# Pairing the blocks: two first products, then two second products, in a fused attention and feed-forward kernel

## The chip, the cores and the metric

One core of a Trainium2 chip runs the kernel. The metric is the device time of one execution in microseconds, the median of three. PE is TensorE (matmul), PEld its weight loads, DVE is VectorE, ACT ScalarE, POOL GpSimd, SP SyncE, whose queue issues the DMAs.

## The reference

Sparse attention over 8 batches, 8 heads, 576 tokens and head size 64, and a feed-forward layer on its output (4608 tokens, 512 channels, 2048 hidden), all in float32:

```python
scores = scale * np.matmul(q, k.transpose(0, 1, 3, 2))
mask_local = (rel >= 0) & (rel < stride)                # heads 0 to 3, stride 32
mask_strided = (rel >= 0) & (pos[None, :] % stride == pos[:, None] % stride)   # heads 4 to 7
attn = softmax(where(mask, scores, -1e9)); x = attn @ v   # tokens x 512
h = x @ w_in
g = 0.5 * h * (1.0 + erf(h * inv_sqrt2))
return (g @ w_out)
```

## The kernel before

**Tiles and steps.** The 4608 tokens are cut into 12 tiles of 384 (`TT`), the hidden layer into 16 blocks of 128 (`NF`). A step n is one hidden block of one tile (t = n // 16, f = n % 16); there are 192 (`NS`). Float32 products are made of three: each factor is split into a high part and a rest (`xh`, `xl`; `gh`, `gl`; `w[:, 0]`, `w[:, 1]`), and three of the four products of parts are added.

- `ffn_h(n)` (L645 to L647) is the first product of a step, called H here: 12 matmuls of 384 columns into one PSUM bank. There are two such banks (`ps_h`, bufs=2), so H(n+2) writes the bank of H(n).
- `ffn_g(n)` is what follows on it: gelu in place (ACT, L654), the cast to `gh` (ACT, L656) and the subtract to `gl` (DVE, L658), which is the last to read the bank. `gh` and `gl` have three buffers each (`gpool`, bufs=3).
- `ffn_o(n)` (L684 to L686) is the second product, called O: 9 matmuls of 512 columns, three into each of three banks that add up over the 16 steps of a tile. `store(t)` (L691) copies the three banks on ACT and sends them out.

**Attention beside it.** The local heads of a tile are three jobs (`band_job`), each in numbered parts: 0 scores (PE, L322), 1 mask and maximum (DVE, L336), 2 exponentials (ACT, L340), 3 sum, quotient, transpose and eight small DMAs (DVE L343 to L346, SP L351), 4 the product with v (PE, L362), 5 and 6 the split into `xh` and `xl` (ACT L263, DVE L265). Parts 4 of one tile and 0 of the next stand together in a *visit*, once a tile. `value_at` and `score_at` say at which step; `soft_at` spreads parts 1 to 3 of the three jobs over the steps behind it. `load_keys` and `load_values` ask for the next tile's data on SP, each held until a gelu named by the caller.

The strided heads are done on DVE alone, as a list of small operations (L520 products, L562 sums) in order (`strided`). `run_strided(upto)` issues the list as far as a planned sum of costs; what a step gets follows from the time left to the tile that needs it, less `taken`, the planned cost of the local heads' vector work. Their exponentials on ACT (L530) wait in `exps` until `flush_exps`; finished outputs wait in `splits` for their split into `xh` and `xl`.

**Order.** An opening (`START`, a list written by hand) loads and splits the weights and does the first 16 steps. From step 16 on `step(n)` is called for each n: visit if there is one, H(n) with all of `ffn_g(n)`, loads, splits, `softmaxes(n)`, the strided share, then O(n−2). On PE this reads H(n), O(n−2), H(n+1), O(n−1), and so on. ACT and PE keep the written order (`manual_schedule`); DVE, POOL and SP are ordered by the scheduler's own timeline. After step 191 one more region does O(190) and O(191) together, bank by bank.

Of the kernel before, what the change touches and what calls it, by code (L numbers as in the profile page):

```python
# [46 lines left out]
NB = 16  # L47
# [35 lines left out]
def attn_ffn_kernel(ctx: ExitStack, tc: tile.TileContext, qk, vl, qka, va, qs, ks, vs, w, out):  # L83
# [6 lines left out]
    NF = w.shape[0]  # L90
    NC = DM // P
    NU = len(PLACE)
    NV = len(VISITS)
    NTILE = NT // TT
    NS = NTILE * NF
    JPT = NJ // NTILE
# [30 lines left out]
    def slot(name, shape, dtype=F32):  # L127

        return wpool.tile(shape, dtype, name=name, tag="w")
# [58 lines left out]
    def set_jq(x):  # L188
        jq[x] = qbig[:, x % JPT]

    def set_jv(x):
        jv[x] = vbig[:, x % JPT].rearrange("p (a h d) -> p a h d", a=2, h=HL)
# [13 lines left out]
    def load_keys(t, after):  # L206

        js = range(t * JPT, (t + 1) * JPT)
        ins = nc.sync.dma_start(qbig, qk[js[0]:js[0] + JPT].rearrange("j p c -> p j c"))
        for x in js:  # L210
            set_jq(x)
        tc.add_manual_dep(ins.ins, after.ins.name, mybir.DependencyInfo(
            mybir.DependencyClass.Sync, mybir.DependencyReason.DATA), reason="pace")

    def load_values(t, after):

        js = range(t * JPT, (t + 1) * JPT)
        ins = nc.sync.dma_start(vbig, vl[js[0]:js[0] + JPT].rearrange("j p a h d -> p j (a h d)"))
        for x in js:
            set_jv(x)  # L220
        tc.add_manual_dep(ins.ins, after.ins.name, mybir.DependencyInfo(
            mybir.DependencyClass.Sync, mybir.DependencyReason.DATA), reason="pace")
# [81 lines left out]
    def score_banks(t):  # L304
        return [ps_a.tile([P, DM], F32, name=f"S{j}_{t}", tag=f"S{j}") for j in range(2)]
# [166 lines left out]
    for vi in range(NA, NV):  # L472
        n = VISITS[vi][2]
# [26 lines left out]
    exps, splits = [], []  # L500

    def flush_exps(u):
        while exps and exps[0][0] <= u:
            exps.pop(0)[1]()
# [131 lines left out]
    hps, gs, ops_, gelu = {}, {}, {}, {}  # L636
    ready = [t * NF for t in range(NTILE)]
    xfree = [0, 0] + ready[1:-1]

    def ffn_h(n):  # L640
        t, f = divmod(n, NF)
        xh, xl = xt[t]
        hp = ps_h.tile([P, TT], F32, name=f"H_{n}", tag="H")
        for c in range(NC):
            nc.tensor.matmul(hp, w1[f][:, 0, c, :], xh[:, c, :], start=(c == 0), stop=False)  # L645
            nc.tensor.matmul(hp, w1[f][:, 0, c, :], xl[:, c, :], start=False, stop=False)  # L646
            nc.tensor.matmul(hp, w1[f][:, 1, c, :], xh[:, c, :], start=False, stop=(c == NC - 1))  # L647
        hps[n] = hp

    def ffn_g(n):  # L650
        hp = hps.pop(n)
        gh = gpool.tile([P, TT], F32R, name=f"gh_{n}", tag="gh")
        gl = gpool.tile([P, TT], F32R, name=f"gl_{n}", tag="gl")
        gelu[n] = nc.scalar.activation(hp, hp, AF.Gelu)  # L654
        yield
        nc.scalar.copy(gh, hp)  # L656
        yield
        nc.vector.tensor_tensor(gl, hp, gh.bitcast(F32), ALU.subtract)  # L658
        gs[n] = (gh, gl)

    def runs(t, a):

        res = []
        for c in range(0, P, 32):
            _, b, r = ROWS[TR * t + (a * P + c) // 32]
            r = b * S + 32 * r
            if res and res[-1][2] + res[-1][1] - res[-1][0] == r:
                res[-1][1] = c + 32
            else:
                res.append([c, c + 32, r])  # L670
        return res

    def ffn_o(*ns):

        t = ns[0] // NF
        if ns[0] % NF == 0:
            ops_[t] = [ps_o.tile([P, DM], F32, name=f"O_{t}_{a}", tag=f"O{a}") for a in range(TT // P)]
        for a in range(TT // P):
            o = ops_[t][a]
            sl = slice(a * P, (a + 1) * P)  # L680
            for n in ns:
                f = n % NF
                gh, gl = gs[n]
                nc.tensor.matmul(o, gh[:, sl], w2[f][:, 0, :], start=(f == 0), stop=False)  # L684
                nc.tensor.matmul(o, gh[:, sl], w2[f][:, 1, :], start=False, stop=False)  # L685
                nc.tensor.matmul(o, gl[:, sl], w2[f][:, 0, :], start=False, stop=(f == NF - 1))  # L686

    def store(t):
        for a in range(TT // P):
            ob = opool.tile([P, DM], F32, name=f"ob_{t}_{a}", tag="ob", bufs=3)  # L690
            nc.scalar.copy(ob, ops_[t][a])  # L691
            for c0, c1, r0 in runs(t, a):
                nc.sync.dma_start(out[r0:r0 + c1 - c0, :], ob[c0:c1, :])
# [5 lines left out]
    for u in range(U0, NU + 1):  # L699
        for v, what, names in ((u, strided_qk, "qk"), (u - 1, strided_av, "v")):  # L700
            if U0 <= v < NU:
                vi, _, r0, nr, t, _ = PLACE[v]
# [11 lines left out]
    def run_strided(upto):  # L714
        while pos[0] < len(strided) and cum[pos[0]] <= upto + 1e-9:
            if strided[pos[0]][1] == 0.6 and len(splits) >= 3:
                break
            strided[pos[0]][2]()
            pos[0] += 1

    for h in range(HL):
        m = smask[h * 32:(h + 1) * 32]
# [19 lines left out]
    t = slot("pbig", [P, 4 * DM])  # L742
# [27 lines left out]
    for i in range(JPT):  # L770
        t = opool.tile([P, DM], F32, name=f"first_{i}", tag="ob", bufs=3)
# [51 lines left out]

    FIRST, VISIT, DELAY = 2, 13, 1
    value_at = {ready[t - 1] + VISIT: t for t in range(2, NTILE)}
    score_at = {ready[1] + FIRST: 2, **{n: t + 1 for n, t in value_at.items()}}
    soft_at = {}
    for n, t in score_at.items():  # L830
        for i in range(JPT if t < NTILE else 0):
            for p in (1, 2, 3):
                soft_at.setdefault(n + p + i * (2 if t == 2 else 4), []).append((t * JPT + i, p))

    taken = [2.2 * (n in value_at) + sum({1: 0.66, 3: 1.2}.get(p, 0) for _, p in soft_at.get(n, ()))
             for n in range(NS + 2)]
# [7 lines left out]
    def part(x, *which):  # L844

        for p in which:
            if p == 0:
                local[x] = [band_job(x, bts[x % NBT], banks), 0]
            assert local[x][1] == p
            local[x][1] += 1  # L850
            next(local[x][0], None)

    def visit(n):

        t = value_at.get(n, 0)
        if score_at.get(n, 0):
            banks[score_at[n]] = score_banks(score_at[n])
        for i in range(JPT if t else 0):
            part(t * JPT + i, 4)
        for i in range(JPT if score_at.get(n, NTILE) < NTILE else 0):  # L860
            part(score_at[n] * JPT + i, 0)

    def softmaxes(n):

        t = value_at.get(n, 0)
        for p in (5, 6) if t else ():
            for i in range(JPT):
                part(t * JPT + i, p)
        for x, p in soft_at.get(n, ()):
            if p == 2:  # L870
                flush_exps(NU)
            part(x, p)

    def step(n):


        c = n // NF
        visit(n)
        if NB <= n < NS:
            ffn_h(n)  # L880
            for _ in ffn_g(n):
                pass
        if n - DELAY in score_at and score_at[n - DELAY] + 1 < NTILE:
            load_keys(score_at[n - DELAY] + 1, gelu[n])
        if n - DELAY in value_at and value_at[n - DELAY] + 1 < NTILE:
            load_values(value_at[n - DELAY] + 1, gelu[n])
        old = len(splits)
        while old and n >= xfree[splits[0][0]]:
            for _ in splits.pop(0)[1]():
                pass  # L890
            old -= 1
        softmaxes(n)
        flush_exps(NU)
        if c + 1 < NTILE:
            a, e = ready[c] + (1 if c == 0 else 0), ready[c + 1]
            part_of = min(1.0, max(0.0, (n - a + 1) / (e - a - 3)))
            need = last[c] + (last[c + 1] - last[c] + sum(taken[a:e - 3])) * part_of - sum(taken[a:min(n + 1, e - 3)])
            share = (n + 1 - NB) / (ready[-1] - 2 - NB)
            run_strided(max(need, (tot + sum(taken)) * share - sum(taken[:n + 1])))
        if n == NS + 1:  # L900
            ffn_o(n - 3, n - 2)
        elif n >= NB + 2 and n < NS:
            ffn_o(n - 2)
        if n >= NB + 2 and (n - 2) % NF == NF - 1:
            store((n - 2) // NF)

    with tc.manual_schedule(engines={ET.Activation, ET.PE}):
        for n in range(NB, NS + 1):
            step(n)
    with tc.manual_schedule(engines={ET.Activation, ET.PE}):  # L910
        step(NS + 1)


def lay_out(q, k, v, w_in, w_out):
# [62 lines left out]
```

## Time and profile before

| | |
|---|---|
| median of 3 runs | 874.68 us (874.24 to 876.21) |
| the profiled execution | 874.25 us, span 872.5 us |
| PE, PEld busy | 855.5, 769.5 us |
| DVE, ACT, POOL busy | 705.9, 483.2, 17.5 us |
| granted TensorE clock, mean | 0.994 |

The span is what the profile sees from the first to the last instruction. Rows of groups give line, engine, operation, output and inputs by name with their shapes, count, then busy time and mean ns of one, then idle time before them and what ended it. Rows of the timeline give start and length in us, engine, line and operation. Rows of stretches give start:end, length, busy time of PE, PEld, DVE, ACT and POOL, the granted clock, the DMA share and GB/s. Rows of waits give who waited for whom: total us, times, longest. Rows of DMA issues give count, KB each and us to landing.

### The profile page before, as it was taken

The page shows a single profiled execution, that of the slowest core. Times are in us where ns is not written, and L with a number is a line of the kernel's source. Part 1 is how long each engine was busy: PE and PEld are TensorE (multiplying, and loading weights), DVE is VectorE, ACT ScalarE, POOL GpSimd, SP SyncE. Part 2 cuts the span into 40 slices and gives each one's busy share as a digit, 9 for nine tenths or more (in the row PEclk, how much of TensorE's full clock was granted, in tenths as well). Part 3 has the DMA queues.
Part 4 walks back from the last instruction along what each step waited for, and adds up shares of the span by engine and source line. Part 5 has one row for each costly group of instructions (what it writes and reads, how often), then busy time and mean ns, then how long its engine had stood idle before and what let it go on. Part 6 is the DMA issues. An engine that isn't in the chain of part 4 may idle for free.

```text
span 872.5 us, 19562 instructions
## 1 busy us (share of the span) xinstructions
PE 855.5 (98%) x6082; PEld 769.5 (88%) x6082; DVE 705.9 (81%) x4901; ACT 483.2 (55%) x1001; POOL 17.5 (2%) x89
## 2 busy tenths in 40 slices
PE   6899999999999999999999999999999999999998
PEld 5788899899899899899899989989989989989997
DVE  5988999998989997889999979899799995751111
ACT  6978586476466466356455546547536535543222
POOL 5000100000000000000000000000000000000000
PEclk9799999999999999999999999999999999999999
DMA  9696210420310150030122121122014003000001
GB/s 345 231 353 229 91 48 19 128 76 8 116 56 9 33 169 8 18 121 19 56 76 73 56 75 48 35 67 98 13 30 141 17 8 93 12 7 16 22 0 37
DMA packets 33976, 66.67 MB, mean 76 GB/s; under 512 B 6224, under 2 KB 15952, under 8 KB 33872
## 3 DMA queue, kind: packets, MB, share of 16 engines
q1 hardware_dynamic: 33872, 65.43, 22.4%
q8 instruction: 48, 0.79, 0.4%
q14 instruction: 56, 0.46, 0.2%
HBM read 51.64 MB, written 9.44 MB: 70 GB/s over the span
## 4 chain that ended last, share of the span: by engine, by line
PE 90%; DMA 4%; DVE 2%; ACT 1%; SPq 1%; issue 1%; ACTq 0%
PE H L645 15%; PE O L685 15%; PE O L686 15%; PE H L647 14%; PE H L646 14%; PE O L684 14%; DMA ws<-in_w_dram 2%; PE X_L L362 1%; PE S L322 1%; DMA qka<-in_qka_dram 1%; DMA sk<-in_ks_dram 1%; SPq L351 1%; PE S L362 1%; DVE w L165 0%; DVE ws L161 0%
## 5 line engine op out<-in xcount | busy, mean ns | idle before, releaser
L654 ACT ACTIVATE H<-H 128x384 f32<-128x384 f32 x192 | 91.3, 476 | 357.4 <-PE H L647 312.4
L645 PE MATMUL H<-xh,w 128*128 128x384 f32 x768 | 260.9, 340 | 1.5 <-DVE gl L658 1.4
L647 PE MATMUL H<-xh,w 128*128 128x384 f32 x768 | 259.7, 338 | 0.0
L646 PE MATMUL H<-xl,w 128*128 128x384 f32 x768 | 258.8, 337 | 0.5 <-DVE xl L265 0.5
L562 DVE SCALAR_TENSOR_TENSOR acc<-sv,sc,acc 128x64 f32<-128x64 f32 x1158 | 249.5, 275 | 0.7
L686 PE MATMUL O<-w,gl 128*128 128x512 f32 x576 | 228.2, 396 | 0.5 <-DVE gl L658 0.5
L685 PE MATMUL O<-w,gh 128*128 128x512 f32 x576 | 227.4, 395 | 0.0
L684 PE MATMUL O<-w,gh 128*128 128x512 f32 x576 | 224.3, 389 | 0.0
L520 DVE CUSTOM_DVE_ANT_0 junk<-sq,sk 128x64 f32<-128x64 f32 x1290 | 204.1, 216 | 1.9 <-DMA sk<-in_ks_dram 1.7
L658 DVE TENSOR_TENSOR gl<-H,gh 128x384 fp32r<-128x384 f32 x192 | 105.7, 551 | 101.2 <-ACT gh L656 100.3
L645 PEld LDWEIGHTS H<-xh,w 128*128 128x128 f32 x768 | 144.9, 189 | 11.0 <-DVE gl L658 1.7
L646 PEld LDWEIGHTS H<-xl,w 128*128 128x128 f32 x768 | 144.7, 188 | 8.7 <-DVE xl L265 0.9
L647 PEld LDWEIGHTS H<-xh,w 128*128 128x128 f32 x768 | 144.6, 188 | 0.1
L686 PEld LDWEIGHTS O<-w,gl 128*128 128x128 f32 x576 | 108.0, 187 | 24.8 <-DVE gl L658 1.7
L685 PEld LDWEIGHTS O<-w,gh 128*128 128x128 f32 x576 | 108.0, 187 | 18.2
L684 PEld LDWEIGHTS O<-w,gh 128*128 128x128 f32 x576 | 108.2, 188 | 17.3
L520 DVE DVE_READ_ACCUMULATOR2_ANT sc<- 128x1 f32 x1290 | 103.3, 80 | 0.0
L656 ACT CAST gh<-H 128x384 fp32r<-128x384 f32 x192 | 92.2, 480 | 6.1
L654 ACT ACT_TABLE_LOAD x60 | 77.0, 1283 | 1.1
L530 ACT ACT_TABLE_LOAD x35 | 44.9, 1283 | 0.6
L340 ACT ACTIVATE PT_L<-P_L,nm_L 128x64 f32<-128x64 f32 x132 | 44.2, 336 | 0.3
L340 ACT ACT_TABLE_LOAD x24 | 30.8, 1283 | 0.5
(114 smaller groups left out, 490.5 us busy)
## 6 DMA issues: line engine op xcount, KB each, us to landing
ws<-in_w_dram SPq DMA_DIRECT2D x16, 1023.8 KB, 9.6
out_dram<-ob SPq DMA_DIRECT2D x34, 256.0 KB, 2.4
qk_all<-in_qk_dram SPq DMA_DIRECT2D x9, 960.0 KB, 5.2
vl_all<-in_vl_dram SPq DMA_DIRECT2D x9, 576.0 KB, 6.7
sk<-in_ks_dram SPq DMA_DIRECT2D x8, 576.0 KB, 5.1
sv<-in_vs_dram SPq DMA_DIRECT2D x8, 576.0 KB, 3.7
band<-PT_L SPq DMA_DIRECT2D x240, 16.0 KB, 1.8
qk_all<-in_qk_dram SPq DMA_DIRECT2D x9, 320.0 KB, 7.7
```

Of the source, the lines that this page charges most:

```text
L340: nc.scalar.activation(pv[:, :, h, :], p1[:, h * 2 * QB:(h + 1) * 2 * QB].rearrange("p (c t) -> p c t", c=2), AF.Exp, bias=nm[:, h:h + 1], ...
L520: nc.vector.tensor_tensor_reduce(junk, sq[vi, "q"][:, r0 + r, :], sq[vi, "k"][:, c, :], 1.0, 0.0, ALU.mult, ALU.add, ss[u][:, r, c:c + 1])
L562: nc.vector.scalar_tensor_tensor(acc[:, r, :], sq[vi, "v"][:, c, :], wgt, acc[:, r, :], ALU.mult, ALU.add)
L645: nc.tensor.matmul(hp, w1[f][:, 0, c, :], xh[:, c, :], start=(c == 0), stop=False)
L646: nc.tensor.matmul(hp, w1[f][:, 0, c, :], xl[:, c, :], start=False, stop=False)
L647: nc.tensor.matmul(hp, w1[f][:, 1, c, :], xh[:, c, :], start=False, stop=(c == NC - 1))
L654: gelu[n] = nc.scalar.activation(hp, hp, AF.Gelu)
L656: nc.scalar.copy(gh, hp)
L658: nc.vector.tensor_tensor(gl, hp, gh.bitcast(F32), ALU.subtract)
L684: nc.tensor.matmul(o, gh[:, sl], w2[f][:, 0, :], start=(f == 0), stop=False)
L685: nc.tensor.matmul(o, gh[:, sl], w2[f][:, 1, :], start=False, stop=False)
L686: nc.tensor.matmul(o, gl[:, sl], w2[f][:, 0, :], start=False, stop=(f == NF - 1))
```

## The change

`step` is replaced by `pair`, called for n = 16, 18, ... 190. It issues, on PE, H(n), H(n+1), O(n−2), O(n−1). Between them:

- the visit stands at the pair's begin; its step is 12 of 16 instead of 13, so that it is even;
- `ffn_g(n)` and the strided share of n follow H(n); gelu of n+1 follows H(n+1);
- loads are asked for behind that gelu (no `DELAY`);
- O(n−2) is issued, then the cast and the subtract of n+1, then splits and the softmax parts of both steps, then the strided share of n+1, then O(n−1) and, where a tile ends, the store.

For tile 2, whose scores are made at step 18, the three jobs' softmax parts start one step apart instead of two. The end is two calls, `ffn_o(NS - 2, NS - 1)` and `store`.

```diff
-    FIRST, VISIT, DELAY = 2, 13, 1
+    FIRST, VISIT = 2, 12
...
-                soft_at.setdefault(n + p + i * (2 if t == 2 else 4), []).append((t * JPT + i, p))
+                soft_at.setdefault(n + p + i * (1 if t == 2 else 4), []).append((t * JPT + i, p))
...
+    def pair(n):
+
+        assert n % 2 == 0 and NB % 2 == 0 and VISIT % 2 == 0 and FIRST % 2 == 0
+        visit(n)
+        ffn_h(n)
+        for _ in ffn_g(n):
+            pass
+        part_strided(n)
+        ffn_h(n + 1)
+        g = ffn_g(n + 1)
+        next(g)
+        if score_at.get(n, NTILE) + 1 < NTILE:
+            load_keys(score_at[n] + 1, gelu[n + 1])
+        if value_at.get(n, NTILE) + 1 < NTILE:
+            load_values(value_at[n] + 1, gelu[n + 1])
+        if n >= NB + 2:
             ffn_o(n - 2)
+        for _ in g:
+            pass
+        old = len(splits)
+        while old and n + 1 >= xfree[splits[0][0]]:
+            for _ in splits.pop(0)[1]():
+                pass
+            old -= 1
+        for m in (n, n + 1):
+            softmaxes(m)
+            flush_exps(NU)
+        part_strided(n + 1)
+        if n >= NB + 2:
+            ffn_o(n - 1)
+            if (n - 1) % NF == NF - 1:
+                store((n - 1) // NF)
 
     with tc.manual_schedule(engines={ET.Activation, ET.PE}):
-        for n in range(NB, NS + 1):
-            step(n)
+        for n in range(NB, NS, 2):
+            pair(n)
     with tc.manual_schedule(engines={ET.Activation, ET.PE}):
-        step(NS + 1)
+        ffn_o(NS - 2, NS - 1)
+        store(NTILE - 1)
```

`part_strided(n)` is the strided share as it stood in `step`, unchanged.

More of the change, by code (lines that the diff above doesn't have):

```diff
@@ L872, in softmaxes, with part_strided @@
             part(x, p)
-    def step(n):
+    def part_strided(n):
         c = n // NF
[L878 to L893, printed above, removed]
         if c + 1 < NTILE:
@@ L899, in step @@
             run_strided(max(need, (tot + sum(taken)) * share - sum(taken[:n + 1])))
-        if n == NS + 1:
-            ffn_o(n - 3, n - 2)
-        elif n >= NB + 2 and n < NS:
-            ffn_o(n - 2)
-        if n >= NB + 2 and (n - 2) % NF == NF - 1:
-            store((n - 2) // NF)
+    def pair(n):
[13 more added lines that the diff above has]
+        if n >= NB + 2:
+            ffn_o(n - 2)
+        for _ in g:
[13 more added lines that the diff above has]
+                store((n - 1) // NF)
     with tc.manual_schedule(engines={ET.Activation, ET.PE}):
-        for n in range(NB, NS + 1):
-            step(n)
+        for n in range(NB, NS, 2):
+            pair(n)
     with tc.manual_schedule(engines={ET.Activation, ET.PE}):
-        step(NS + 1)
+        ffn_o(NS - 2, NS - 1)
+        store(NTILE - 1)
 def lay_out(q, k, v, w_in, w_out):
```

## The prediction

> **What bounds the kernel now.** I read the page's busy line first, then the chain that ended last, then the stretches of 50 us, then PE's waits, and last single rows of the timeline.
>
> ```profile
> span 872.5 us, 19562 instructions
> PE 855.5 (98%) x6082; PEld 769.5 (88%) x6082; DVE 705.9 (81%) x4901; ACT 483.2 (55%) x1001; POOL 17.5 (2%) x89
> ...
> PE H L645 15%; PE O L685 15%; PE O L686 15%; PE H L647 14%; PE H L646 14%; PE O L684 14%; DMA ws<-in_w_dram 2%; PE X_L L362 1%; PE S L322 1%; DMA qka<-in_qka_dram 1%; DMA sk<-in_ks_dram 1%; SPq L351 1%; PE S L362 1%; DVE w L165 0%; DVE ws L161 0%
> ```
>
> The chain is the two products (H and O, 87% together). The stretches and PE's waits say where PE ever stood:
>
> ```profile
> 100.00:150.00 50.00, 50.00 (x343) 45.21 (x342) 48.93 (x440) 34.77 (x70) 0.28 (x2) 1.00 0.14 44
> 150.00:200.00 50.00, 50.00 (x383) 45.15 (x382) 47.77 (x351) 29.34 (x60) 0.50 (x4) 1.00 0.29 91
> ```
>
> ```profile
> PE S L322 <- DMA qk_all<-in_qk_dram: 4.6, 1, 4.6
> ...
> PE H L645 <- DVE gl L658: 1.4, 1, 1.4
> PE H L646 <- DVE xl L265: 0.5, 1, 0.5
> PE O L686 <- DVE gl L658: 0.5, 1, 0.5
> ```
>
> From 100 us on PE is busy 50.00 of 50.00 at full clock (1.00), so nothing it waits for sets the time there; its few waits lie in the opening, which the diff leaves alone. The time can fall only if the same matmuls run closer together, and can rise only through a wait that is not there now. VectorE is the engine to watch: 48.93 and 47.77 of 50 us in these stretches.
>
> So the question is what a row of matmuls costs by its place. Starts of PE's instructions at the end (the last first-product block, one ordinary second-product block, then the 18 second products that already stand behind it today):
>
> ```profile
> 860.12 0.33 PE L645 MATMUL H<-xh,w 128*128 128x384 f32 x1
> ...
> 862.23 0.39 PE L684 MATMUL O<-w,gh 128*128 128x512 f32 x1
> ...
> 864.31 0.39 PE L684 MATMUL O<-w,gh 128*128 128x512 f32 x1
> ...
> 868.16 0.39 PE L686 MATMUL O<-w,gl 128*128 128x512 f32 x1
> ```
>
> A first-product block takes 862.23 − 860.12 = 2.11 us, a second-product block behind it 864.31 − 862.23 = 2.08 us: 4.19 us a step, 231 ns for each of the nine O matmuls. The next 18 stand 17 starts apart in 868.16 − 864.31 = 3.85 us: 226.5 ns each, so nine of them take 2.04. Second products that follow second products are 0.04 us cheaper per nine. These 18 also begin with new subtracts to wait on, so a satisfied wait does not bring the dearer pace back.
>
> For first products the nearest pair of rows is two visits, one with O before it (156.16 on) and one where the block before was H (107.28 on):
>
> ```profile
> 107.28 1.17 PE L322 MATMUL S<-qk_all 64*32 64x64 f32 x96
> 108.38 0.44 PE L645 MATMUL H<-xh,w 128*128 128x384 f32 x1
> 108.66 0.34 PE L646 MATMUL H<-xl,w 128*128 128x384 f32 x1
> ...
> 110.57 0.39 PE L684 MATMUL O<-w,gh 128*128 128x512 f32 x1
> ```
>
> ```profile
> 156.16 1.17 PE L322 MATMUL S<-qk_all 64*32 64x64 f32 x96
> 157.26 0.44 PE L645 MATMUL H<-xh,w 128*128 128x384 f32 x1
> 157.54 0.33 PE L646 MATMUL H<-xl,w 128*128 128x384 f32 x1
> ...
> 159.47 0.39 PE L684 MATMUL O<-w,gh 128*128 128x512 f32 x1
> ```
>
> From the second matmul to the first O are 11 starts: 110.57 − 108.66 = 1.91 us where H came before, 159.47 − 157.54 = 1.93 where O came before. At 1.91/11 = 174 ns twelve take 2.08 against the ordinary 2.11. So first products behind first products are about 0.026 us cheaper.
>
> **The change, part by part.**
>
> *Two and two.* Before, each H and each O follows the other kind. After, in each pair from n = 18 to 190 the second H follows an H and the second O an O: 87 pairs. Saving per pair: 2.11 − 2.084 = 0.026 and 2.08 − 2.04 = 0.041, together 0.067 us; times 87 = 5.8 us. By two-decimal rows each part is known to about ±0.01, so 4.5 to 7 us. Nothing hides it, since PE has no idle time to take it. No matmul is added: 12 and 9 per step as before, and the last 18 second products are the same call.
>
> By the Trainium skill's page "TensorE: Matmul & The Clock Gate" ("Back-to-back issue gap") the warm gap of a matmul is its columns over 2.4 GHz plus 2.5 ns, whatever stands before it. By that rule order is worth nothing and the saving is 0; the rows above, 231 and 226.5 ns for one shape, do not agree with it.
>
> *The second cast and subtract.* gh and gl have three buffers, so the cast of step n+1 must wait for the second product of n−2, which now stands right after H(n+1) and before stood ahead of it. How long a block needs to be finished with on ACT and VectorE:
>
> ```profile
> 118.48 0.56 DVE L658 TENSOR_TENSOR gl<-H,gh 128x384 fp32r<-128x384 f32 x1
> 118.94 0.39 PE L684 MATMUL O<-w,gh 128*128 128x512 f32 x1
> 119.14 0.47 ACT L654 ACTIVATE H<-H 128x384 f32<-128x384 f32 x1 [2.79 <-PE H L647]
> 119.64 0.48 ACT L656 CAST gh<-H 128x384 fp32r<-128x384 f32 x1
> 121.02 0.33 PE L645 MATMUL H<-xh,w 128*128 128x384 f32 x1
> ```
>
> Gelu starts 0.20 us after the block's last start, the cast ends at 1.18, and a subtract of 0.55 could end at 1.8. For the odd step the cast begins 2.08 + 0.20 after H(n+1) and the subtract can end at about 3.3. The bank is needed by H(n+3), after O, O and H: 2.08 + 2.04 + 2.11 = 6.2. Spare: 2.9 us; for the even step 4.4 as before. ACT is held for some 1.3 us per pair by this wait; behind it stand the split copies and the exponentials of the pair's tail, which no matmul of that pair reads.
>
> But VectorE does not take the subtract at once. The odd subtract of n = 19 (first row) ends at 119.04 and H(21) starts at 121.02: 1.98 us ahead. If VectorE's order and times stay, H(n+3) now comes one H block (2.11) sooner, which leaves −0.13. The worst odd one:
>
> ```profile
> 653.29 0.55 DVE L658 TENSOR_TENSOR gl<-H,gh 128x384 fp32r<-128x384 f32 x1
> 654.57 0.33 PE L645 MATMUL H<-xh,w 128*128 128x384 f32 x1
> ```
>
> It ends 0.73 us ahead of H(143), so −1.4. One more of that kind would bring the bound to about 3 us of stalls plus restarts (a first matmul after other work shows 0.28 against 0.17 to the next start, so 0.1 each): ends 0 and 3.5 us. I take 0.5, near the first row: the local heads' work goes behind the odd subtract, and each stall lets VectorE catch up, so stalls of one stretch do not add.
>
> *Softmaxes in the tail.* The exponentials (part 2) fall on even steps and the rest (part 3) on the next odd one, now issued one behind the other. VectorE's waits now:
>
> ```profile
> DVE ss_L L343 <- ACT PT_L L340: 17.3, 20, 2.2
> DVE z L546 <- ACT sc L530: 16.2, 21, 1.0
> ```
>
> The 20 waits on the exponentials cost 0.9 us each, 2.2 at most. VectorE's order is the scheduler's, and the strided share of n+1 follows to fill the gap. On the path: 0, so long as the spare times above hold; without that cover it is the slower rival. For tile 2 the three jobs come a step apart instead of two; `taken` subtracts their planned cost from the strided share, so the same work sits closer together: 0.
>
> *Visit at step 12, no DELAY.* The visits number the same and their matmuls are the same rows (156.16 to 157.26 and the two small ones ahead). Keys and values are asked for a step earlier on SP, 16 steps (67 us) ahead of use, and the band copies issued after them start well before the next visit:
>
> ```profile
> qk_all<-in_qk_dram SPq DMA_DIRECT2D x9, 960.0 KB, 5.2
> vl_all<-in_vl_dram SPq DMA_DIRECT2D x9, 576.0 KB, 6.7
> band<-PT_L SPq DMA_DIRECT2D x240, 16.0 KB, 1.8
> ```
>
> All land within 7 us: 0. Between the visit and the tile that needs its x now lie four steps, not three.
>
> *Store.* The three copies now stand behind the last O of a tile and ahead of two H blocks (4.2 us), not one (2.1), before that bank is written again: 0, with more room. The last region issues the same matmuls; only the cast of n = 191 waits for O(188), and O(189) (2.04) covers its cast and subtract (about 1.3).
>
> **Sum.** −5.8 + 0.5 = −5.3 us. The profiled execution took 874.25 (span 872.5 and 1.75 around it); the median shown is 874.68, 0.43 above, and the saving is taken from that: 869.3, which I give as 869.2.
>
> **The rivals.**
>
> *Part of it goes into stalls (870.5 to 873).* For it: the −0.13 and −1.4 above, and 97% busy VectorE, which gets 0.067 us less per pair. Against: most subtracts end 2 to 4 us ahead. With the whole 3.5: 874.7 − 5.8 + 3.5 = 872.4.
>
> *The order does not matter (874.7), or for one kind only.* If the dear start belongs to a block and not to the change of kind, nothing is saved. For it: the visit rows differ by only 0.02, at the edge of what they resolve; the second-product rows come from the end, where VectorE has little to do. Only O gives 874.7 − 87 × 0.041 = 871.1, only H 872.4. By the gap rule of the Trainium skill, named above, the time would end at that 874.7.
>
> *Slower (about 880).* VectorE stands at part 3 until the exponentials are through, and all behind it, the even subtract among it, is late. Three jobs a tile in the four fullest tiles, 12 waits at the 2.2 us of the longest, make 26 us; VectorE's room in the two stretches above is (1.07 + 2.23) of 100 us, so 9 us of 4 × 67. That leaves 17 of stalls and 874.7 − 5.8 + 17 = 886; at 1.6 us a wait, 879. It decides from about 1.4 us each on (12 × 1.4 = 17, against 9 + 5.8 + 1.75). Against: 0.9 is the mean now, and the even subtract has 4.4 us of room. That VectorE takes its queue strictly in order is what the same page of the Trainium skill says under "Engine queue depths"; the waits above, during which VectorE is idle, fit that.
>
> **How the numbers follow.** Forecast (868.2 to 870.5) 0.60; partly stalled (870.5 to 873) 0.17; one kind only 0.06 and neither 0.06; slower 0.11. The range 868.2 to 873.2 takes in the first two and the one-kind case, some 8 in 10; the likeliest case's own range is 868.2 to 870.5. A measurement of this kernel tells a change from none at about 0.2%, 1.75 us: faster means below 872.9 (0.60 + nearly all of 0.17 + 0.06 = 0.82), the same 0.07, slower 0.11.
>
> **What would show it.** Right: nine O matmuls of the second block at 2.04 us, the second H block at 2.08, pairs of 8.31 us against 2 × 4.19, PE still at 50.00 of 50 from 110 us on, the cast of odd steps 2.3 us after its H. Wrong: a wait of H on gl in PE's list, above all at odd steps between 110 and 250 us or near 650; longer waits of VectorE on ss_L; or four blocks that all keep 2.11 and 2.08.

## The result: slower, 884.6 us

| | median | runs | profiled execution | its span |
|---|---|---|---|---|
| before | 874.46 us | 874.22 to 876.21 (4) | 874.25 us | 872.5 us |
| after | 884.63 us | 881.37 to 886.40 (4) | 886.40 us | 884.6 us |

The ratio is 1.0108, with a 95% interval of 1.0072 to 1.0143. The page of the changed kernel, the lines that answer those shown of before:

```profile
span 884.6 us, 19601 instructions
PE 855.3 (97%) x6082; PEld 770.6 (87%) x6082; DVE 705.0 (80%) x4901; ACT 462.6 (52%) x985; POOL 17.6 (2%) x89
...
PE 75%; DVE 14%; DMA 6%; ACT 3%; issue 1%; SPq 1%; ACTq 0%; DVEq 0%
...
L645 PE MATMUL H<-xh,w 128*128 128x384 f32 x768 | 262.4, 342 | 11.4 <-DVE gl L658 11.3
```

The chain by engine, before:

```profile
PE 90%; DMA 4%; DVE 2%; ACT 1%; SPq 1%; issue 1%; ACTq 0%
```

The work is the same; PE now stands idle. VectorE, which had 2% of the chain, has 14%, and the first matmul of H blocks waited 11.3 us for gl. Three stretches of the changed kernel, then PE's waits from 107 us on:

```profile
107.00:250.00 143.00, 136.24 (x1019) 122.98 (x1019) 125.24 (x1008) 76.21 (x161) 1.11 (x8) 0.96 0.21 67
250.00:500.00 250.00, 247.36 (x1638) 223.89 (x1637) 227.52 (x1720) 136.19 (x298) 1.64 (x12) 1.00 0.17 55
500.00:750.00 250.00, 249.05 (x1776) 225.44 (x1775) 221.47 (x1658) 125.28 (x277) 1.51 (x11) 1.00 0.17 54
```

```profile
PE H L645 <- DVE gl L658: 10.3, 7, 4.3
```

Most of the loss lies before 250 us (143.00 − 136.24 = 6.8 us of idle PE, and a granted clock of 0.96). Yet where PE does not wait, the pairs are what the forecast said. A pair near 120 us (first H, second H, first O, second O, next pair):

```profile
118.98 0.33 PE L645 MATMUL H<-xh,w 128*128 128x384 f32 x1
...
121.08 0.33 PE L645 MATMUL H<-xh,w 128*128 128x384 f32 x1
...
123.16 0.39 PE L684 MATMUL O<-w,gh 128*128 128x512 f32 x1
...
125.24 0.39 PE L684 MATMUL O<-w,gh 128*128 128x512 f32 x1
...
127.28 0.33 PE L645 MATMUL H<-xh,w 128*128 128x384 f32 x1
```

The blocks take 2.10, 2.08, 2.08 and 2.04 us, 8.30 in all. What goes wrong is first seen at step 24. PE, ScalarE and SP there, each from its own timeline:

```profile
143.67 0.39 PE L686 MATMUL O<-w,gl 128*128 128x512 f32 x1
148.38 0.69 PE L645 MATMUL H<-xh,w 128*128 128x384 f32 x1 [4.33 <-DVE gl L658]
148.87 0.52 PE L646 MATMUL H<-xl,w 128*128 128x384 f32 x1
149.19 0.52 PE L647 MATMUL H<-xh,w 128*128 128x384 f32 x1
```

```profile
133.57 0.48 ACT L656 CAST gh<-H 128x384 fp32r<-128x384 f32 x1 [0.93 <-PE O L685]
142.71 1.28 ACT L340 ACT_TABLE_LOAD   x1 [8.66 <-DMA band<-PT_L]
...
146.75 0.47 ACT L654 ACTIVATE H<-H 128x384 f32<-128x384 f32 x1
```

```profile
135.74 10.57 SPq L351 DMA_DIRECT2D band<-PT_L  x16
```

Read from the bottom: SP issues the eight small copies of job 0 and of job 1 of tile 2, 16 in 10.57 us, 0.66 us each. ScalarE wants to write the exponentials of job 2 into the buffer `PT` that job 0 used (there are two), and job 0's copies still read it. It stands for 8.66 us, from 134.05 on: 1.7 us pass before the first copy leaves (VectorE's part 3 of job 0 ends only at 135.68), the eight copies of job 0 then start one behind the other until 140.1, and the rest is the landing of the last. Behind it stands the gelu of H(24): that block's last matmul starts at 137.52, its gelu only at 146.75. So gl(24) is late, H(26) waits 4.33 us, and then its matmuls stand 0.32 us apart instead of 0.174: the granted clock is 0.50 from 149 to 153 us.

That the clock drops after idle time is also in the Trainium skill, "TensorE: Matmul & The Clock Gate", "Part 1: The HAM clock gate", which names a window of about 3.4 us without work and then half the rate. Here 4.33 us did it, as that says; but a wait of 2.16 us that ended at 172.48 was followed by slow matmuls as well, from the eighth on (granted clock 0.50 from 174 to 177 us).

### The profile page after: what moved, and what is told of

It is laid out like the page before. It is cut to its first block, busy times and chain, and to the rows that moved or that the text cites. A ratio compares the mean times of both kernels' runs of the same rounds, so it can differ in the third digit from the quotient of the medians.

```text
span 884.6 us, 19601 instructions
## 1 busy us (share of the span) xinstructions
PE 855.3 (97%) x6082; PEld 770.6 (87%) x6082; DVE 705.0 (80%) x4901; ACT 462.6 (52%) x985; POOL 17.6 (2%) x89
## 4 chain that ended last, share of the span: by engine, by line
PE 75%; DVE 14%; DMA 6%; ACT 3%; issue 1%; SPq 1%; ACTq 0%; DVEq 0%
PE H L645 13%; PE H L646 12%; PE H L647 12%; PE O L685 12%; PE O L686 12%; PE O L684 12%; DVE acc L562 6%; DVE junk L520 4%; DMA ws<-in_w_dram 3%; DMA vl_all<-in_vl_dram 2%; DVE gl L658 1%; ACT L530 1%; PE X_L L362 1%; ACT PT_L L340 1%; DMA sk<-in_ks_dram 1%
## 5 line engine op out<-in xcount | busy, mean ns | idle before, releaser
L645 PE MATMUL H<-xh,w 128*128 128x384 f32 x768 | 262.4, 342 | 11.4 <-DVE gl L658 11.3
L686 PE MATMUL O<-w,gl 128*128 128x512 f32 x576 | 226.5, 393 | 0.7 <-DVE gl L658 0.7
L560 DVE TENSOR_SCALAR acc<-sv,sc 128x64 f32<-128x64 f32 x132 | 25.8, 246 | 0.7 <-DMA sv<-in_vs_dram 0.3
```

## The experiments

Theory A had two parts: the buffer `PT`, held by copies that leave one by one, stops ScalarE at step 24; and behind visits the scheduler puts too much strided work between a cast and its subtract. The rivals named the cast behind O(n−2), the visit at step 12 by itself, and a VectorE that is simply full. All ratios are against the kernel before, run on the same chip in the same batch; two kernels of different batches are better compared by their ratios than by their medians.

**One figure back: two steps of spacing.**

```diff
-                soft_at.setdefault(n + p + i * (1 if t == 2 else 4), []).append((t * JPT + i, p))
+                soft_at.setdefault(n + p + i * (2 if t == 2 else 4), []).append((t * JPT + i, p))
```

> The changed kernel with one figure put back: the softmax parts of tile 2's three jobs start two steps apart, as before the change, not one. Theory A (the third job's exponentials need the buffer PT of the first, which is held until its eight small copies, issued by SP at 0.63 us each, have landed; ScalarE is held 8.7 us at step 24, H(26) waits 4.5 us and the clock drops): that wait and the cold matmuls near 148 us go, 4.5 us of wait and about 2 us of slow clock; the median falls from 884.6 to about 878, and the waits behind the visits (1 to 2.5 us each) stay. Rival B (ScalarE is held by the second cast, which waits for O(n-2)): spacing is nothing, 884 to 885.

Measured 881.96 us (ratio 1.0081, 1.0053 to 1.0108). The hold of ScalarE is gone, and so far theory A is right, but 2.7 us came back where it said 6 to 7. PE's waits from 95 us on:

```profile
PE H L645 <- DVE gl L658: 3.3, 3, 1.4
PE S L362 <- DMA band<-PT_L: 2.7, 2, 2.0
PE X_L L362 <- DMA band<-PT_L: 2.5, 1, 2.5
```

5.2 us are new: the visit now stands at step 28, and with two steps of spacing the third job's bands land after it has begun. Behind these waits the granted clock is 0.50 from 153 to 162 us. So the spacing of one belongs to the visit at step 12; either figure for it costs a wait.

**That figure alone, in the old kernel.**

```diff
-                soft_at.setdefault(n + p + i * (2 if t == 2 else 4), []).append((t * JPT + i, p))
+                soft_at.setdefault(n + p + i * (1 if t == 2 else 4), []).append((t * JPT + i, p))
```

> The kernel before with that one figure alone: tile 2's jobs one step apart. Theory A: the buffer and the eight copies are the same in the old order, so ScalarE is held by the same 8 us or so near step 23 or 24 and H(n+2) waits 2 to 6 us: 877 to 882. Rival B (it needs the pairs): no change, 874.2 to 875.2.

Measured 880.16 us (ratio 1.0063, 1.0044 to 1.0082), as theory A said. ScalarE's and PE's waits:

```profile
ACT L340 <- DMA band<-PT_L: 6.2, 1, 6.2
```

```profile
PE H L645 <- DVE gl L658: 4.2, 1, 4.2
```

The pairs have no part in this hold: it costs about 6 us in the old order too.

**The pairs undone on PE, the rest kept.** H(n), O(n−2), H(n+1), O(n−1), with two steps of spacing:

```diff
         part_strided(n)
+        if n >= NB + 2:
+            ffn_o(n - 2)
         ffn_h(n + 1)
...
-        if n >= NB + 2:
-            ffn_o(n - 2)
         for _ in g:
```

> The changed kernel with tile 2's jobs two steps apart and PE's order inside a pair put back to H(n), O(n-2), H(n+1), O(n-1); visit at step 12, the loads, the place of the softmaxes and the strided share stay as changed. Theory A (the waits behind the visits come from the odd subtract, whose bank is wanted one H block sooner in the paired order): the waits go or shrink below 1 us in all, the 5.8 us of saving go too: 874 to 876, PE's wait list from 110 us on nearly empty. Rival C (the visit at step 12 and the softmaxes behind the second subtract make VectorE late by themselves): the waits of H on gl stay, 3 us or more, 877 to 882.

Measured 882.06 us (ratio 1.0085, 1.0066 to 1.0104), outside what either theory gave. PE's waits tell why:

```profile
PE S L362 <- DMA band<-PT_L: 3.4, 2, 2.0
PE X_L L362 <- DMA band<-PT_L: 2.2, 1, 2.2
PE H L645 <- DVE gl L658: 0.2, 1, 0.2
```

The waits of H on gl are nearly gone (0.2 us), which is theory A's second part. The odd subtract still comes late (at step 93 it starts 4.13 us behind the end of its cast), but only the paired order wants its bank so early that H waits. The time is that of the old order plus the late bands (5.6 us) and, behind them, a granted clock of 0.50 from 155 to 161 us.

**VectorE in the written order.** With two steps of spacing; part 3 of a softmax is moved behind the strided share of the odd step (`softmaxes` is given a second argument, the parts to issue; that hunk is left out here):

```diff
...
-        for m in (n, n + 1):
-            softmaxes(m)
-            flush_exps(NU)
+        softmaxes(n)
+        softmaxes(n + 1, (1, 2))
+        flush_exps(NU)
         part_strided(n + 1)
+        softmaxes(n + 1, (3,))
...
-    with tc.manual_schedule(engines={ET.Activation, ET.PE}):
+    with tc.manual_schedule(engines={ET.Activation, ET.PE, ET.DVE}):
         for n in range(NB, NS, 2):
```

> The changed kernel with tile 2's jobs two steps apart and VectorE, too, kept in the written order from step 16 on (the scheduler's timeline orders it in the changed kernel); part 3 of a softmax is written behind the strided share of n+1, not ahead of it, so that VectorE does not stand before the exponentials. Theory A (the subtracts behind a visit are late because the scheduler puts up to 7 us of strided work between cast and subtract): each subtract starts within 3 us of its cast, H waits under 1 us in all, and the 5.8 us of the paired order show: 868.5 to 871. Rival D (VectorE has too little room whatever its order): waits on gl of several us stay, 875 or more.

Measured 873.57 us (ratio 0.9991, 0.9981 to 1.0002), no difference from before. No wait of H on gl is left; the one wait from 95 us on is the bands':

```profile
PE S L362 <- DMA band<-PT_L: 2.6, 2, 2.2
```

So VectorE is not too full. The run changes two things, the written order and the place of part 3; which of them it takes is seen in the runs with the third buffer below. The number missed the forecast by the bands and the slow clock behind them (0.50 from 154 to 160 us).

**A third buffer, all else as changed.** The third job's exponentials go into the space of a tile that only the opening uses:

```diff
-        p2 = lpool.tile([P, DM], F32, name=f"PT_L{x}", tag="PT", bufs=2)
+        p2 = (lpool.tile([P, DM], F32, name=f"PT_L{x}", tag="lead", bufs=1) if x >= 2 * JPT and x % JPT == 2
+              else lpool.tile([P, DM], F32, name=f"PT_L{x}", tag="PT", bufs=2))
```

> The changed kernel with a third buffer for the third job's exponentials (it takes the space of a tile that only the opening uses); spacing, order and all else as changed. Theory A (the hold at step 24 is that buffer, kept until the first job's eight copies have landed): ScalarE's 8.7 us hold and the 4.5 us wait of H(26) go, and with them the slow clock near 148 us; tile 2's bands are there before the visit at step 28, unlike with two steps of spacing; the waits of H on gl behind visits stay: 876 to 880. Rival B (the cast behind O(n-2) holds ScalarE): 884 to 885.

Measured 872.50 us (ratio 0.9979, 0.9968 to 0.9991): 12.1 us below the changed kernel, more than theory A said, and now slightly faster than before. PE's waits from 95 us on:

```profile
PE H L646 <- DVE gl L659: 2.1, 3, 0.9
```

One buffer of 2 KB a partition takes back the whole loss against before; by the two ratios (1.0108 and 0.9979) it is worth 11.3 us. The hold cost more than its own 4.3 us: the slow clock went with it, and so did the waits of H(30) and H(31), 2.4 us, for subtracts that started 6.7 us behind their casts. Not all of the difference is the hold. The scheduler's order of VectorE changed as well: the waits of H(94), H(95) and H(111), 2.7 us together in the changed kernel, are gone, and H(46) and H(49) wait 1.2 us instead.

**The third buffer and VectorE's written order, part 3 left where the change put it.** The `manual_schedule` line of the run "VectorE in the written order", on top of the third buffer.

> The kernel of the row above, and VectorE kept in the written order from step 16 on, with part 3 of a softmax where the changed kernel writes it, ahead of the strided share of the odd step. Theory A (the scheduler's order alone makes the subtracts late): no subtract is more than 4 us behind its cast, but VectorE stands before the exponentials, up to 2 or 3 us for each of 30 jobs; there is room for some of it, so 868.5 to 873. The rival of the prediction (VectorE standing before part 3 makes the kernel slower): 876 or more, with H waiting on gl in the full tiles.

Measured 871.85 us (ratio 0.9964, 0.9948 to 0.9979). PE's waits, then VectorE's:

```profile
PE H L646 <- DVE gl L659: 1.4, 2, 0.8
```

```profile
DVE ss_L L344 <- ACT PT_L L341: 16.2, 16, 1.8
```

VectorE does stand before the exponentials, 1.0 us each of 16 times; PE's waits come to 1.4 us, not to the 10 and more of the slower rival. The written order by itself is worth too little to tell from the run above: 0.9964 against 0.9979, with intervals that overlap.

**All three: third buffer, written order, part 3 late.**

> All three together: third buffer, VectorE in the written order, part 3 behind the strided share. Theory A: no wait of PE from 110 us on, pairs of 8.31 us throughout, and the 5.8 us of the paired order: 868 to 869 beside 873.7 to 874.5 of the kernel before. Rival D (another wait takes their place, as the bands did with two steps of spacing): 871 or more.

Measured 867.63 us (867.41 to 867.77; ratio 0.9921, 0.9906 to 0.9936), the fastest version of this study. The same three stretches as above:

```profile
107.00:250.00 143.00, 143.00 (x998) 130.18 (x986) 132.37 (x1019) 83.97 (x180) 1.05 (x8) 1.00 0.20 62
250.00:500.00 250.00, 249.92 (x1781) 226.16 (x1780) 230.39 (x1664) 132.81 (x286) 1.75 (x13) 1.00 0.18 56
500.00:750.00 250.00, 250.00 (x1655) 227.13 (x1654) 228.95 (x1696) 128.02 (x286) 1.37 (x10) 1.00 0.19 57
```

PE is busy all along (0.08 us apart). In the changed kernel the cast and the subtract of the visit's step 76 stand 4.19 us apart (377.30 to 381.49). Those of the odd step 77 stand 4.10 apart (380.78 to 384.88), and for that subtract H(79) waits:

```profile
376.82 0.48 ACT L656 CAST gh<-H 128x384 fp32r<-128x384 f32 x1
...
381.49 0.55 DVE L658 TENSOR_TENSOR gl<-H,gh 128x384 fp32r<-128x384 f32 x1
...
385.48 0.44 PE L645 MATMUL H<-xh,w 128*128 128x384 f32 x1 [0.89 <-DVE gl L658]
```

In the fastest version both subtracts follow their casts within 0.05 us; step 76:

```profile
362.15 0.48 ACT L657 CAST gh<-H 128x384 fp32r<-128x384 f32 x1
362.66 0.56 DVE L659 TENSOR_TENSOR gl<-H,gh 128x384 fp32r<-128x384 f32 x1 [1.49 <-ACT gh L657]
```

The median is 4.2 us below that of the run above, the profiled execution 2.0 us; PE's waits account for 1.4 of it.

**The same with the pairs undone on PE.**

> The kernel of the row above with PE's order in a pair put back to H(n), O(n-2), H(n+1), O(n-1): the worth of two and two by itself, when nothing waits. Theory A (0.041 us for each second O, 0.026 for each second H, 87 pairs): 5.8 us more than the row above, 873.7 to 875. Rival E (order is worth nothing, and the rows of the trace mislead): the same as the row above within 0.5 us.

Measured 873.87 us (ratio 0.9998, 0.9987 to 1.0010), and PE has no wait from 95 us on here either. 873.87 − 867.63 = 6.2 us is what two and two are worth when nothing waits. Between the two profiled executions (spans 872.4 and 865.6) it is 6.8 us, of which 1.4 lie in the opening, which the order does not touch: 5.4. The forecast's 5.8 lies between 5.4 and 6.2.

**Starts 0, 1 and 3 steps behind the scores, two buffers.**

```diff
-                soft_at.setdefault(n + p + i * (1 if t == 2 else 4), []).append((t * JPT + i, p))
+                soft_at.setdefault(n + p + ((0, 1, 3)[i] if t == 2 else i * 4), []).append((t * JPT + i, p))
```

> The changed kernel, tile 2's three jobs starting 0, 1 and 3 steps behind step 18 instead of 0, 1 and 2; two buffers, as changed. A dose of the buffer's hold: the third job's exponentials come one step (4.2 us) later against copies that need 8 x 0.63 us, and its bands still land ahead of the visit at step 28. Theory A: ScalarE's hold of 8.7 us shrinks by about 4 us, H(26) waits under 1 us, no slow clock; what is left are the waits behind visits: 872 to 877, near the kernel with three buffers (872.5). Rival F (the third buffer helped by moving the scheduler's order, not by the hold): 880 or more.

Measured 882.40 us (ratio 1.0091, 1.0071 to 1.0111), and ScalarE's hold did not shrink:

```profile
ACT L340 <- DMA band<-PT_L: 8.9, 1, 8.9
```

The dose was none. The exponentials moved from step 22 to step 23, but both are written in the tail of the same pair, so ScalarE reaches them at the same time. This run does not speak for rival F, for which only the 1.5 us of changed waits in the run with the third buffer speak; it shows that in the paired code a move by one step can be no move.

**Half of the copies from GpSimd's queue**, from tile 2 on; one step of spacing, two buffers:

```diff
-                nc.sync.dma_start(bt[kb * QB:(kb + 1) * QB, g, :], tv[g * QB:(g + 1) * QB, c, :])
+                (nc.gpsimd if c and x >= 2 * JPT else nc.sync).dma_start(
+                    bt[kb * QB:(kb + 1) * QB, g, :], tv[g * QB:(g + 1) * QB, c, :])
```

> The changed kernel with one change in the copies: from tile 2 on, of a job's eight copies four are issued by SP and four by GpSimd, so that they leave in half the time; spacing of one step, two buffers. Theory A (issue on SP, 0.63 us each, makes the hold long): the hold of ScalarE at step 24 shrinks from 8.7 us by 2 to 4, H(26) waits 0 to 2.5 us, 873 to 880. Rival G (the hold is the copies' flight, or ScalarE waits on something else): the hold stays within 1 us and the time at 882 to 886.

Measured 873.78 us (ratio 0.9991, 0.9978 to 1.0004). The hold:

```profile
ACT L340 <- DMA band<-PT_L: 5.8, 1, 5.8
```

2.9 us shorter, as theory A said. H(26) starts 1.85 us behind the start of the last O instead of 4.71, no slow matmul follows, and the median is 10.8 us lower (10.2 by the ratios). The issue of the copies, one after another, is thus a good part of the hold; the 5.8 us that are left are not split further.

**Starts 0, 1 and 3 with the written order.**

> The first row's starts (0, 1 and 3 steps) with VectorE in the written order and part 3 behind the strided share of the odd step; two buffers, so no memory is borrowed. Theory A (three things cost time: the hold, bands that land after the visit, and the scheduler's late subtracts; nothing else): no wait of PE from 110 us on, 867 to 869, as with three buffers (867.6). Rival: one of the three is not cured by this, 870 or more.

Measured 871.26 us (ratio 0.9965, 0.9953 to 0.9977), above the forecast: a hold of 5.2 us is left (the move by one step is no move in the paired code, as the first run of these starts showed), and PE waits 1.6 us on gl and 0.4 on a band. The third buffer is the cleaner cure.

## Why the prediction was wrong

**Right: the saving by order.** (The sum, 874.68 − 5.3 = 869.4, was given as 869.2; nothing hangs on that.) 0.067 us a pair and 5.8 us in all, by 231 and 226.5 ns for the same O matmul. The blocks of the changed kernel show 2.08 and 2.04, and the two kernels that differ in the order alone stand 6.2 us apart. The rival "the order does not matter" is out. With it goes the gap rule of the Trainium skill, "TensorE: Matmul & The Clock Gate", "Back-to-back issue gap", as a rule for this kernel: that section gives its formula for an isolated matmul, says that in a stream the weight loads set the spacing too, and has no term for what stood before.

**Wrong: the step "Softmaxes in the tail", for tile 2.** It says that "`taken` subtracts their planned cost from the strided share, so the same work sits closer together: 0". It counted VectorE's time only. The step that was moved also issues exponentials into one of two buffers and eight copies on SP, and neither the ring of two nor SP's 0.6 us a copy was counted. Instead of 0 this term measured 11 to 12 us (884.63 − 872.50 = 12.1, 11.3 by the ratios), of which some 1.5 is the scheduler's changed order and not the hold. The prediction shows the row `band<-PT_L`, 240 issues on SP, and reads from it only that a copy lands in 1.8 us. SP's timeline of before shows what the eight copies of one job take:

```profile
129.28 4.96 SPq L351 DMA_DIRECT2D band<-PT_L  x8
```

That is longer than the step of 4.19 us that was left.

**Wrong in part: the step "Visit at step 12".** "The band copies issued after them start well before the next visit" holds for spacing one. With two steps, the old spacing, PE waited 2.6 to 5.6 us for bands in the visit at step 28, in three runs. The two edits were priced at 0 each. The earlier visit needs the closer spacing, and the closer spacing runs into the buffer, with the old visit too (880.16 us).

**Mis-sized: the odd subtract.** The mechanism was as told: H(n+3) comes one H block sooner and waits on gl. 0.5 us was taken, with 3.5 as the far end; without the hold it measured 2.1 us of idle PE, 1.5 of it at H(49) and H(79), for odd subtracts, and 0.6 at H(46), for an even one, to which the prediction had given 4.4 us to spare. The hope that moving the local heads' work behind the odd subtract would help did not hold: at the visits of steps 28 to 124 the scheduler leaves 2.6 to 6.7 us between cast and subtract (step 76: 4.19). With the written order and part 3 moved it is 3.3 us at most, at any step, and no H waits. Why the scheduler orders so is not shown; that its own timeline takes visits for longer than they are would fit, and was not tried.

**The slower rival named the wrong engine.** It had VectorE wait for the exponentials. Those waits did not grow from the 17.3 us of before; in the changed kernel they are:

```profile
DVE ss_L L343 <- ACT PT_L L340: 16.2, 22, 2.2
```

ScalarE, held by a DMA queue, was not among the rivals.

Part of the 12.1 us between the two profiled executions is the opening, which the diff leaves alone. The first visit's scores, in the changed kernel and then in the fastest one:

```profile
109.48 1.17 PE L322 MATMUL S<-qk_all 64*32 64x64 f32 x96
```

```profile
105.95 1.17 PE L322 MATMUL S<-qk_all 64*32 64x64 f32 x96
```

Before it was 107.28. The same opening thus varies by some 3.5 us between these executions, and 2.2 us of what the profile of the changed kernel shows above that of before is this.

## What to carry to other kernels

An edit that moves a step moves everything the step issues: ask of each buffer in its ring who still reads the last content, and of each queue how long its issues take in series, before setting the price to zero. When a PE-bound kernel gets slower, look for the engine in front of the last releaser: H waited on VectorE, VectorE on ScalarE, ScalarE on a DMA, and only that last wait named the cause. And a gain found by counting starts can be real while the whole change loses; kernels that differ in one edit each told the two apart.

## What the runs showed of the hardware

- The spacing of starts depends on what came before: nine matmuls of 512 columns take 2.08 us behind the other product's block and 2.04 behind their own kind; twelve of 384 columns 2.11 and 2.08. What makes the difference inside PE is not shown.
- Small copies issued by one queue leave about 0.63 us apart (eight in 4.96 us before, 16 in 10.57 in the changed kernel), although one lands in 1.8; a second queue shortened the hold they caused from 8.7 to 5.8 us.
- Idle time of little more than 2 us was enough to be followed by matmuls at 0.32 us instead of 0.174. From 107 us on, each PE wait of 2.07 us or more in these runs was followed by, or fell into, a stretch with a granted clock of 0.50 (2.16 us in the changed kernel, 2.07 with starts 0, 1 and 3), and waits of up to 1.46 us, where no longer one stood near them, were not.
